# Two attention and GeGLU layers on one core: the second layer's first unit handled in two halves of its queries, other banks for dense products at the seam, new planner settings

## The chip, the core and the metric

The kernel runs on one core of a Trainium2 chip. Its engines each run their own instruction stream and meet through semaphores: TensorE (PE in the profile; its weight loads are shown as PEld) does the matrix products and writes PSUM, VectorE (DVE) and ScalarE (ACT) read PSUM, GpSimd (POOL) works on SBUF alone, and SyncE (SP) starts the DMAs. PSUM has eight banks of 512 fp32 columns. The metric is device time in microseconds of one launch; lower is better.

## What is computed

Two identical layers, each of attention with 32 heads of width 16 over 2048 tokens and a GeGLU feed-forward block. Everything is bf16 outside the accumulations.

```python
def _A_ref(x, wqkv, wo):          # H = 32, Dh = 16
    q, k, v = ...                 # x @ wqkv, split into heads
    scores = jnp.einsum("bhqd,bhkd->bhqk", q, k) * (Dh ** -0.5)
    p = _softmax(scores, axis=-1)
    o = jnp.einsum("bhqk,bhkd->bhqd", p, v)
    return o.transpose(0, 2, 1, 3).reshape(B, S, D) @ wo

def _B_ref(x, w_gate, w_up, w_down):
    return (_gelu(x @ w_gate) * (x @ w_up)) @ w_down

x = A_x                            # 1 x 2048 x 512; F = 1792
x = x + _A_ref(_layernorm(x), A_wqkv, A_wo)
x = x + _B_ref(_layernorm(x), B_w_gate, B_w_up, B_w_down)
x = x + _A_ref(_layernorm(x), A_wqkv, A_wo)
x = x + _B_ref(_layernorm(x), B_w_gate, B_w_up, B_w_down)
```

## The kernel before

**Units.** The queries of a layer are cut into blocks (four of 512 in the first layer; three of 512 and two of 256 in the second), the heads into eight groups of four. A block and a group make a unit. The four heads of a group lie in four row strips of 32 partitions, so a score product uses a quarter of PE's rows and two or four of them run side by side.

**Two passes.** A softmax subtracts the maximum of each row. The first pass finds it: `p1_emit` (L1636 matmul, L1651 DVE maximum) takes 128 queries, one key block of 512 and one head at a time, called a tile below; one maximum covers two tiles that lie in two neighbouring banks (128x1024) or a single one (128x512). A unit of 512 queries has 64 tiles, a layer 2048. When all tiles of a unit are done, `fin_step` reduces the four key blocks' maxima in six POOL steps (L1004 to L1009), DVE transposes the result (L1015), and `negmax` sends it by four small DMAs (L1031) into an extra row of QT, so that the second pass's scores come with the maximum subtracted. The second pass, `p2_tile` (L1518 matmul) and `p2_emit` (L1495 exponential on ACT, usually of two banks at once), makes the probabilities, and `pv_emit` (L1541) multiplies them with the values into bank 7; `nrm` divides by the sum. `QT`, `KT` and `KD` hold queries, keys and differences of two key blocks.

**Folds.** ACT can take a part of the first pass: `f_emit` (L1468 matmul with KD, L1475 ACT Relu) forms the positive part of a difference of two tiles, and DVE's L1646 adds it to the other tile while it takes the maximum, so that one 128x512 instruction serves two tiles.

**Dense products.** Projections, the output product and the feed-forward block are matmuls over all 128 rows (L759), made in runs of PIECE or GP matmuls between score matmuls. Each takes a free bank from `misc_banks` and is evicted by DVE or ACT; `pick` chooses (L774, L776). PE also issues filler matmuls on zeros (L1669) where it would stand idle.

**Banks.** The first pass owns banks 0 to 3, the second 4 to 6, the accumulator 7. While a dense product is open or could start, `p1_plan` is asked for its single form, in which the first pass uses the pair 0 and 1 and the single bank 2, and `misc_banks` hands out bank 3; where the second pass has nothing to do, 4 to 6 as well.

**The order** is worked out on the host: a planner (the loop at the end of `_build`) walks through time by estimates of each instruction's duration and emits the next instruction of every engine. Its choices are ruled by 19 settings (look-ahead, lag between the passes, size of runs, which engine evicts, and so on), which it takes from a row of PLAN; a new row is read after each 16 pairs of tiles (STRETCH).

**The seam between the layers.** The second layer's keys need the first layer's last feed-forward block. Therefore the first six units of the second layer (n_pre = 6) run over the first three key blocks of each group before any of them sees the fourth; `p1_turn` puts the rest in order of units as soon as the last key block of the first group is there. The first pass may be at most six units ahead of the second (n_ahead = 6), and the second pass can start only when the first unit is finished:

```python
if not p1_left[u]:                              # p1_emit
    fin_wait.append({"u": u, "stage": 0})
...
if u >= NU or u not in qp2_rec or gel["on"] is not None:   # p2_group
    return None
...
if pl is not None and (opened or fresh or wide) and not (gel["on"] is not None and (run or not fresh)):
    pl = p1_plan(now, True)
```

Here `can_p2` is false while the second pass has no unit to work on and `can_p1` true while the first pass has one; `gel["on"]` is set while the last block's gate products run with the Gelu on ACT; `pos["p1"]` counts pairs of tiles.

Of the kernel before, what the change touches and what calls it, by code (L numbers as in the profile page):

```python
# [11 lines left out]
AP = bass.AP  # L12
# [298 lines left out]
def _build(nc, x_in, wqkv, wo, wg, wu, wd, out, layer_blocks=((512, 512, 512, 512), (512, 512, 512, 256, 256)),  # L311
# [10 lines left out]
    NTT = S // 128  # L322
    NKB = S // 512
# [4 lines left out]
    with es:  # L328
# [138 lines left out]
        held = set()  # L467
# [1431 lines left out]
```

## Time and profile before

| | us |
|---|---|
| median of 3 runs | 2490.07 |
| lowest to highest | 2490.03 to 2490.46 |
| the profiled execution | 2490.04 |
| its span, first to last instruction | 2488.2 |

A profile's page gives one execution: the busy time of each engine and its share of the span, the span in 40 slices with the busy share of each in tenths, and the costliest groups of instructions. A group's row has the line, the engine, the operation, what it writes and reads with its shapes, the count, the busy time and the mean duration of one, and then the idle time just before it with what ended that. Rows of the timeline start with the start time and the duration of one or several merged instructions, of which the first one's shape is shown; a bracket holds the idle time before them and its releaser. Rows of busy time by stage hold the stretch, its length, and for each engine the busy time and the count. Some matmul records can be missing.

### The profile page before, as it was taken

How to read it: one execution, taken by the hardware profiler on the slowest of the kernel's cores; microseconds unless marked ns; L12 is line 12 of the kernel's file. 1: busy time of each engine (PE TensorE's matmuls, PEld its weight loads, DVE VectorE, ACT ScalarE, POOL GpSimd, SP SyncE). 2: the span in 40 equal slices, each digit the busy share in tenths (PEclk: the TensorE clock that was granted, in tenths of full speed). 3: DMA queues.
4: the chain of work that ended last, by engine and by line, in shares of the span. 5: the costliest groups of instructions: out<-in, count | busy, mean ns of one | idle time of the engine just before them, and what ended most of it. 6: DMA issues, size and time to landing. Idle time of an engine off the chain costs nothing.

```text
span 2488.2 us, 68820 instructions
## 1 busy us (share of the span) xinstructions
PE 2383.5 (96%) x29466; PEld 1145.1 (46%) x29720; DVE 2413.9 (97%) x3200; ACT 2340.4 (94%) x3190; POOL 1307.0 (53%) x2156
## 2 busy tenths in 40 slices
PE   8999999999999999999999999999999999999999
PEld 3444444444444444444433555554444444554456
DVE  9999999999999999999999999999999999999994
ACT  7999999999999999999965999999999999999996
POOL 5121238856788356877242211278617882269462
DMA  3110000000000000000000000000000000000000
GB/s 96 46 57 6 6 2 8 2 4 4 4 4 2 3 5 4 4 10 2 17 7 12 5 4 4 4 5 1 2 13 6 2 3 12 4 3 4 9 5 11
DMA packets 27354, 25.11 MB, mean 10 GB/s; under 512 B 9512, under 2 KB 26024, under 8 KB 27048
## 3 DMA queue, kind: packets, MB, share of 16 engines
q1 hardware_dynamic: 27048, 20.69, 2.9%
q8 instruction: 233, 3.82, 0.6%
q14 instruction: 73, 0.60, 0.1%
HBM read 9.70 MB, written 2.10 MB: 5 GB/s over the span
## 4 chain that ended last, share of the span: by engine, by line
DVE 41%; PE 36%; ACT 21%; issue 1%; POOL 0%; POOLq 0%; ACTq 0%; DVEq 0%
DVE PM L1651 39%; ACT SCR L1495 20%; PE PS L1636 12%; PE PS L759 9%; PE PS L1541 8%; PE PS L1518 3%; PE PS L1669 3%; DVE SCR L1646 1%; ACT SCR L1135 0%; ACT SCR L1475 0%; PE PS L881 0%; DVE HT L583 0%; PE PS L1468 0%; ACT AO L1209 0%; DVE AO L1229 0%
## 5 line engine op out<-in xcount | busy, mean ns | idle before, releaser
L1651 DVE TENSOR_REDUCE PM<-PS 128x2 f32<-128x1024 f32 (+1 forms) x2596 | 2234.8, 924 | 30.5 <-PE PS L1636 9.1
L1495 ACT ACTIVATE SCR<-PS 128x1024 bf16<-128x1024 f32 (+1 forms) x2484 | 2028.6, 910 | 69.0 <-PE PS L1518 47.3
L1636 PE MATMUL PS<-KT,QT 32*128 32x512 bf16 x3936 | 1047.0, 385 | 56.5 <-DVE PM L1651 33.4
L1518 PE MATMUL PS<-QT,KT 32*128 32x512 bf16 (+2 forms) x4736 | 945.7, 354 | 6.3 <-ACT SCR L1495 5.1
L1541 PE MATMUL PS<-VP,SCR 128*128 128x51 bf16 (+1 forms) x16384 | 811.3, 187 | 11.3 <-ACT SCR L1495 6.2
L1541 PEld LDWEIGHTS PS<-VP,SCR 128*128 128x128 bf16 x16384 | 573.5, 96 | 497.7 <-issue 421.7
L1636 PEld LDWEIGHTS PS<-KT,QT 32*128 32x128 bf16 x3936 | 249.7, 91 | 531.2 <-DVE PM L1651 328.8
L1669 PE MATMUL PS<-WV,ZER 128*128 128x240 bf16 x1948 | 365.7, 266 | 4.3 <-ACT SCR L1495 3.4
L1059 POOL TENSOR_TENSOR RL<-ACCS,CM 128x16 f32<-128x16 f32 (+2 forms) x66 | 179.4, 2718 | 339.9 <-ACT ACCS L1053 339.5
L1518 PEld LDWEIGHTS PS<-QT,KT 32*128 32x128 bf16 x4736 | 239.2, 91 | 65.9 <-ACT SCR L1495 41.2
L1004 POOL TENSOR_TENSOR PM<-PM 128x32 f32<-128x32 f32 (+2 forms) x74 | 18.0, 243 | 325.9 <-DVE PM L1651 320.6
L1669 PEld LDWEIGHTS PS<-WV,ZER 128*128 128x128 bf16 x1948 | 147.8, 96 | 61.7 <-issue 47.8
L1211 POOL TENSOR_TENSOR HT<-HT,AO 128x512 bf16<-128x512 bf16 x98 | 113.6, 1161 | 103.3 <-ACT AO L1209 102.6
L1248 POOL TENSOR_TENSOR KD<-KT 128x512 bf16<-128x512 bf16 x74 | 85.3, 1153 | 94.1 <-PE PS L1468 54.1
L759 PE MATMUL PS<-XNT,WU 128*128 128x512 bf16 (+2 forms) x499 | 124.4, 333 | 4.2 <-issue 2.9
L759 PE MATMUL PS<-XNT,WG 128*128 128x512 bf16 (+2 forms) x500 | 121.1, 333 | 5.1 <-issue 3.5
L759 PE MATMUL PS<-WD,HT 128*128 128x512 bf16 x384 | 121.2, 381 | 3.3 <-issue 1.4
L1139 POOL TENSOR_TENSOR HT<-HT,SCR 128x512 bf16<-128x512 bf16 (+1 forms) x98 | 106.2, 1083 | 4.7
L1133 POOL TENSOR_TENSOR SCR<-SCR,HT 128x512 bf16<-128x512 bf16 (+1 forms) x98 | 106.0, 1083 | 1.7
L1129 POOL TENSOR_TENSOR SCR<-HT 128x512 bf16<-128x512 bf16 (+1 forms) x98 | 95.8, 978 | 18.2 <-ACT HT L776 12.9
L1646 DVE CUSTOM_DVE_ANT_0 SCR<-PS,SCR 128x512 bf16<-128x512 f32 x160 | 102.7, 686 | 2.8 <-PE PS L1636 1.0
L1475 ACT ACTIVATE SCR<-PS 128x1024 bf16<-128x1024 f32 (+1 forms) x81 | 84.4, 1043 | 19.8 <-PE PS L1468 18.3
(128 smaller groups left out, 1509.1 us busy)
## 6 DMA issues: line engine op xcount, KB each, us to landing
KT<-SG SPq DMA_DIRECT2D x64, 64.0 KB
QT<-SG SPq DMA_DIRECT2D x56, 64.0 KB
QT<-MT SPq DMA_DIRECT2D x224, 1.0 KB
out_dram<-AO SPq DMA_DIRECT2D x16, 128.0 KB, 1.7
WG<-in_B_w_gate_dram SPq DMA_DIRECT2D x4, 448.0 KB, 3.8
WU<-in_B_w_up_dram SPq DMA_DIRECT2D x4, 448.0 KB, 4.8
WD<-in_B_w_down_dram SPq DMA_DIRECT2D x4, 384.0 KB, 4.5
HT<-in_A_x_dram SPq DMA_DIRECT2D x2, 512.0 KB, 8.9
```

Source lines behind the costliest of these rows:

```text
L759: ins = e.matmul(out_ap, lhsT=l, rhs=r_, start=(i == 0), stop=(i == n - 1))
L1059: emit("pool", lambda e: e.tensor_tensor(RL[:, s, 0:4 * nq], lsum, CM1[:, 0:4 * nq], op=ALU.pow), r=[("ACCS", s), ("CM1",)], w=[("RL", s)] ...
L1133: emit("pool", lambda e: e.tensor_tensor(u, u, ht, op=ALU.mult), r=[ku, kh], w=[ku], dur=0.18 + n / 520.0)
L1139: emit("pool", lambda e: e.tensor_tensor(ht, ht, u, op=ALU.mult), r=[ku, kh], w=[kh], dur=0.18 + n / 520.0)
L1211: emit("pool", lambda e, ft=ft, o=o: e.tensor_tensor(HV[:, ft, :], HV[:, ft, :], AO[:, o, 0:n], op=ALU.mult), r=[("AO", o)] + ht_keys(ft, ...
L1495: emit("act", lambda e: e.activation(dst, src, ACTF.Exp, scale=DH ** -0.5), r=[BK[bk + i] for i in range(cnt)], w=[("PT", i) for i in slot ...
L1518: ins = e.matmul(bank(bk)[:, i * n:(i + 1) * n], lhsT=KT[32 * j:32 * j + 32, g, kt * 128:(kt + 1) * 128], rhs=QT[32 * j:32 * j + 32, s, 0: ...
L1541: ins = e.matmul(acc, lhsT=PT[:, slot, i * n + qt * 128:i * n + (qt + 1) * 128], rhs=AP(VP, (kt * H + 4 * g + j) * 17, [[NTT * H * 17, 128 ...
L1636: ins = e.matmul(bank(b), lhsT=QT[32 * j:32 * j + 32, s, qt * 128:(qt + 1) * 128], rhs=KT[32 * j:32 * j + 32, g, kb * 512:(kb + 1) * 512], ...
L1646: emit("dve", lambda e, i=i, b=b, sl=sl: e.tensor_tensor_reduce(PT[:, sl, :], bank(b), PT[:, sl, :], 1.0, -3.0e38, ALU.add, ALU.max, po[:, ...
L1651: emit("dve", lambda e: e.tensor_reduce(po, PS[:, bs[0]:bs[0] + cnt, :], axis=AX.X, op=ALU.max), r=bks, w=[("PM", sm) + h[1:] for h in hs] ...
L1669: return e.matmul(PS[:, b, NACC:512], lhsT=ZER[:, :], rhs=WV[:, 0, 0:512 - NACC], start=(b != 7), stop=(b != 7), skip_group_check=True)
```

## The change

Three things are changed.

1. `qh` gives the number of parts in which a unit is finished: two (QH1) for the first unit of the second layer, one for all others. Tiles are counted per part, `fin_step` and `negmax` work on a part's queries, each part has its own key in the dependence tracking, and the second pass goes through that unit's first 256 queries and then through the others.
2. Past the 64th pair of tiles, while the second pass has nothing to work on, the first pass has, and no Gelu stretch is on, dense products take banks 4 to 6 only, and the first pass keeps its two pairs of banks.
3. 116 of PLAN's 128 rows are new; rows 2, 3, 6 to 11 and 13 to 16 stay.

```diff
 PLAN = [
-    (0.1, 0.0, 0.65, 0.42, 0.3, -0.1, 1, 1, 62, 84, 8, 80, 0.1, 2.0, 0, 2, 2, 2, 7),
-    (0.0, 0.0, 0.65, 0.42, 0.3, 0.05, 1, 1, 62, 160, 8, 80, 0.1, 2.0, 0, 2, 3, 2, 7),
+    (0.1, 0.0, 0.65, 0.42, 0.3, -0.1, 1, 1, 62, 6, 8, 80, 0.3, 2.0, 0, 2, 2, 2, 7),
+    (0.4, 0.05, 0.45, 0.22, 0.0, 0.0, 2, 2, 110, 36, 8, 80, 0.3, 4.0, 0, -6, 1, 4, 6),
...
@@ misc_banks
             if gel["on"] is not None and can_p1[0]:
                 bs = [5, 6] if GF else [4, 5, 6]
+            elif not can_p2[0] and can_p1[0] and pos["p1"] > 64:
+                bs = [4, 5, 6]
             elif not can_p2[0]:
                 bs += ([3] if bmode[0] else []) + [4, 5, 6]
@@ _build
+        qh = {u: 1 for u in range(NU)}
+        for la in range(1, NL):
+            qh[min(u for u in range(NU) if units[u][0] == la)] = QH1
+        qh_left = {(u, h): 16 * units[u][3] // 128 // qh[u] for u in range(NU) for h in range(qh[u])}
+        qh_done = {u: 0 for u in range(NU)}
+
+        def qkey(u, qt):
+            h = qt * qh[u] // (units[u][3] // 128)
+            return ("QT", u % n_qt, h) if h else ("QT", u % n_qt)
+
+        def p2_key(u):
+            return qkey(u, p2["h"] * (units[u][3] // 128) // qh[u])
+
+        def qh_count(u, qt):
+            h = qt * qh[u] // (units[u][3] // 128)
+            qh_left[u, h] -= 1
+            if not qh_left[u, h]:
+                fin_wait.append({"u": u, "stage": 0, "h": h})
@@ fin_step
-            nq = n // 128
-            pm = PM[:, s1, 0:nq * 4 * NKB].rearrange("p (a k) -> p a k", a=nq)
-            keys = [("PM", s1, qt, kb, j) for qt in range(nq) for kb in range(NKB) for j in range(4)]
+            nq = units[u][3] // 128 // qh[u]
+            q0 = f["h"] * nq
+            pm = PM[:, s1, q0 * 4 * NKB:(q0 + nq) * 4 * NKB].rearrange("p (a k) -> p a k", a=nq)
+            keys = [("PM", s1, qt, kb, j) for qt in range(q0, q0 + nq) for kb in range(NKB) for j in range(4)]
@@ negmax
-                        AP(QT, n_qt * 512 + sl * 512 + pg * 32, [[32 * n_qt * 512, 4], [128, nq], [1, 32]]),
+                        AP(QT, n_qt * 512 + sl * 512 + h * nq * 128 + pg * 32, [[32 * n_qt * 512, 4], [128, nq], [1, 32]]),
-            qp2_rec.add(u)
+            qh_done[u] += 1
+            if qh_done[u] == qh[u]:
+                qp2_rec.add(u)
@@ p2_group
-            if u >= NU or u not in qp2_rec or gel["on"] is not None:
+            if u >= NU or qh_done[u] <= p2["h"] or gel["on"] is not None:
                 return None
@@ p2_tile
-                                   rhs=QT[32 * j:32 * j + 32, s, 0:n], start=True, stop=True, tile_position=(32 * j, 0))
+                                   rhs=QT[32 * j:32 * j + 32, s, c0:c0 + n], start=True, stop=True, tile_position=(32 * j, 0))
@@ p1_emit
-            if not p1_left[u]:
-                fin_wait.append({"u": u, "stage": 0})
+            for h in hs:
+                qh_count(u, h[1])
@@ the planner's loop
-                if pl is not None and (opened or fresh or wide) and not (gel["on"] is not None and (run or not fresh)):
+                if pl is not None and (opened or fresh or wide) and not (gel["on"] is not None and (run or not fresh)) \
+                        and not (not can_p2[0] and gel["on"] is None and pos["p1"] > 64 and 3 not in held):
                     pl = p1_plan(now, True)
```

More of the change, by code (lines that the diff above doesn't have):

```diff
@@ L973, in qproj @@
                 sl = (u + i) % n_qt
-                keys = [("QT", sl)]
+                keys = [("QT", sl)] + [("QT", sl, h) for h in range(1, max(qh.values()))]
                 yield ("sp", [("SG", s)], keys)
@@ L1016, in fin_step, with negmax @@
                  r=[("MSEL", u % 2)], w=[("MT", u % 2)], dur=0.13)
-            fin_rec.add(u)
-            add(negmax(u), -1e6 + u)
+            if f["h"] == qh[u] - 1:
+                fin_rec.add(u)
+            add(negmax(u, f["h"]), -1e6 + u)
             f["stage"] = 9
             return True
-        def negmax(u):
+        def negmax(u, h):
             s1 = u % n_ahead
             sl = u % n_qt
-            nq = units[u][3] // 128
-            yield ("sp", [("MT", u % 2)], [("QT", sl)])
+            nq = units[u][3] // 128 // qh[u]
+            key = qkey(u, h * nq)
+            yield ("sp", [("MT", u % 2)], [key])
             def fn(e):
@@ L1366, in p2_group @@
             u = p2["u"]
-            if u >= NU or u not in qp2_rec or gel["on"] is not None:
+            if u >= NU or qh_done[u] <= p2["h"] or gel["on"] is not None:
                 return None
             if p2["todo"] is None:
-                p2["todo"] = [list(range(NTT * units[u][3] // 512)) for j in range(4)]
+                p2["todo"] = [list(range(NTT * units[u][3] // 512 // qh[u])) for j in range(4)]
             return u
@@ L1394, in p2_only @@
                 return []
-            tq = max(est([("QT", p2["u"] % n_qt)]), now)
+            tq = max(est([p2_key(p2["u"])]), now)
             left = p2_left()
@@ L1443, in f_opts @@
                     return []
-                tq = max(est([("QT", h[0] % n_qt), ("KD", h[0] % NKD)]), est(w=[("PT", so)]), now)
+                tq = max(est([qkey(h[0], h[1]), ("KD", h[0] % NKD)]), est(w=[("PT", so)]), now)
                 bs = (4,) if gel["on"] is not None else (6, 5) if wide else (6,)
@@ L1449, in f_opts @@
                 return []
-            tq = max(est([("QT", h[0] % n_qt), ("KD", h[0] % NKD)]), est(w=[("PT", sp), ("PT", sp + 1)]), now)
+            tq = max(est([qkey(h[0], h[1]), ("KD", h[0] % NKD)]), est(w=[("PT", sp), ("PT", sp + 1)]), now)
             return sorted((max(tq, est(w=[BK[b], BK[b + 1]])), b, 2, True) for b in ((3, 5) if wide else (4, 5))
@@ L1472, in f_emit @@
             bks = [BK[bk + d] for d in range(cnt)]
-            emit_pe(fn, 1, 512, r=[("QT", s), ("KD", sd)], w=bks, rows=[j + d for d in range(cnt)])
+            emit_pe(fn, 1, 512, r=[qkey(u, qt), ("KD", sd)], w=bks, rows=[j + d for d in range(cnt)])
             avoid.extend(j + d for d in range(cnt))
@@ L1498, in p2_emit @@
             if not p2_left():
-                p2_done.add(u)
-                p2["u"] += 1
+                p2["h"] += 1
                 p2["todo"] = None
+                if p2["h"] == qh[u]:
+                    p2_done.add(u)
+                    p2["u"] += 1
+                    p2["h"] = 0
         def p2_tile(u, avoid, bk, slot):
@@ L1508, in p2_tile @@
             kg = p2["todo"][j].pop(0)
+            c0 = p2["h"] * n // qh[u]
+            n //= qh[u]
             m = 512 // n
@@ L1518, in fn @@
                     ins = e.matmul(bank(bk)[:, i * n:(i + 1) * n], lhsT=KT[32 * j:32 * j + 32, g, kt * 128:(kt + 1) * 128],
[L1519 removed]
+                                   rhs=QT[32 * j:32 * j + 32, s, c0:c0 + n], start=True, stop=True, tile_position=(32 * j, 0))
                 return ins
[L1522 to L1523 removed]
+            emit_pe(fn, m, n, r=[p2_key(u)] + [("KT", g, kt // 4) for kt in kts], w=[BK[bk]], rows=[j])
+            return u, slot, j, kts, p2["h"]
         def pv_emit():
[L1526 removed]
+            u, slot, j, kts, h = pvq.pop(0)
             la, bi, t0, n, g = units[u]
+            nh = n // qh[u]
+            q0 = h * nh // 128
             first = u in pv_first
@@ L1535, in fn @@
                 for i, kt in enumerate(kts):
-                    for qt in range(nq):
+                    for qt in range(q0, q0 + nh // 128):
                         a = (qt * 4 + j) * 17
@@ L1540, in fn @@
                         acc = AP(PS, 7 * 512 + a, [[8 * 512, 128], [na - a, nb], [1, 17]])
-                        ins = e.matmul(acc, lhsT=PT[:, slot, i * n + qt * 128:i * n + (qt + 1) * 128],
+                        ins = e.matmul(acc, lhsT=PT[:, slot, i * nh + (qt - q0) * 128:i * nh + (qt - q0 + 1) * 128],
                                        rhs=AP(VP, (kt * H + 4 * g + j) * 17, [[NTT * H * 17, 128], [0, nb], [1, 17]]),
@@ L1639, in fn @@
                 return ins
-            emit_pe(fn, 1, 512, r=[("QT", s)] + kks, w=bks, rows=[h[3] for h in hs])
+            emit_pe(fn, 1, 512, r=[qkey(u, qt)] + kks, w=bks, rows=[h[3] for h in hs])
             po = AP(PM, sm * 16 * NKB + (qt * NKB + kb) * 4 + j0, [[n_ahead * 16 * NKB, 128], [1, cnt]])
```

15 lines of the change are left out of this document (6 added, 9 removed), and 226 rows, old and new, of the table PLAN.

## The prediction

> **What bounds the kernel now.** I read the page's head first, then busy time by stage, then the timeline of each engine at the seam between the layers.
>
> ```profile
> span 2488.2 us, 68820 instructions
> ...
> PE 2383.5 (96%) x29466; PEld 1145.1 (46%) x29720; DVE 2413.9 (97%) x3200; ACT 2340.4 (94%) x3190; POOL 1307.0 (53%) x2156
> ...
> ACT  7999999999999999999965999999999999999996
> ```
> ```profile
> 62.20:1240.00 1177.80, 1126.86 (x14053) 535.47 (x14173) 1168.50 (x1465) 1146.78 (x1560) 656.67 (x1094) 1.00 0.04 10
> ...
> 1368.00:1680.00 312.00, 305.56 (x4293) 159.66 (x4303) 305.43 (x396) 311.45 (x347) 102.56 (x191) 1.00 0.02 4
> 1680.00:2426.00 746.00, 714.64 (x9189) 344.12 (x9287) 735.22 (x933) 714.73 (x1031) 450.13 (x677) 1.00 0.02 5
> 2426.00:2488.20 62.20, 57.57 (x903) 39.77 (x907) 26.52 (x70) 43.56 (x82) 16.01 (x34) 1.00 0.03 11
> ```
>
> After the span the columns are PE, PEld, DVE, ACT, POOL. DVE (maxima of the first pass) and ACT (exponentials) share the bound. DVE is idle 9.3 us in the first long stage, 6.6 in the second, 10.8 in the third: 26.7 us over 2236. ACT is idle 31.0, 0.6 and 31.3 there. The large hole is the 6 and 5 in the ACT row: the seam. From 1368 to 1680 ACT is full and DVE has air; from 1680 on it is the other way round. So time won at the seam on ACT alone is worth its full size until 1680, and afterwards only as far as work can be moved from DVE to ACT.
>
> The profiled run took 2490.04 us, 1.84 over its span; the median of the three runs is 2490.07. The sum below starts from 2490.04.
>
> **The halves.** ACT's way out of the seam, then DVE, POOL, SP and PE on the same stretch:
>
> ```profile
> 1347.85 0.60 ACT L776 ACTIVATE VP<-PS 128x512 bf16<-128x512 f32 x1 [1.55 <-PE PS L759]
> 1348.47 1.28 ACT L1495 ACT_TABLE_LOAD   x1
> 1356.74 2.11 ACT L1495 ACTIVATE SCR<-PS 128x1024 bf16<-128x1024 f32 x2 [6.99 <-PE PS L1518]
> ```
> ```profile
> 1339.60 11.80 DVE L1651 TENSOR_REDUCE PM<-PS 128x2 f32<-128x1024 f32 x14 [1.79 <-PE PS L1636]
> 1351.32 0.20 DVE L1015 STREAM_TRANSPOSE MT<-MSEL 128x32 bf16<-128x32 bf16 x1
> ```
> ```profile
> 1349.22 0.25 POOL L1004 TENSOR_TENSOR PM<-PM 128x32 f32<-128x32 f32 x1 [15.78 <-DVE PM L1651]
> ...
> 1350.92 0.23 POOL L1009 TENSOR_TENSOR MSEL<-PM 128x16 bf16<-128x16 f32 x1
> 1358.58 0.25 POOL L1004 TENSOR_TENSOR PM<-PM 128x32 f32<-128x32 f32 x1 [7.43 <-DVE PM L1651]
> ```
> ```profile
> 1336.88 4.95 SPq L938 DMA_DIRECT2D KT<-SG  x8
> 1351.55 10.51 SPq L1031 DMA_DIRECT2D QT<-MT  x6
> ```
> ```profile
> 1356.27 0.39 PE L1518 MATMUL PS<-QT,KT 32*128 32x512 bf16 x2
> ```
>
> The last key block lands (SP), DVE takes unit 0's 16 tiles of 512 keys that lack it from 1339.60 until POOL starts at 1349.22, so 9.6 us or 0.60 a tile. POOL's six steps last to 1351.15, DVE transposes, SP issues four small DMAs at 1351.55, and the first score matmul of the second pass runs at 1356.27, 4.7 us after. With halves, eight tiles suffice: the chain starts 4.8 us earlier and the first exponential comes at 1356.74 − 4.8 = 1351.9. ACT's table load, done at 1349.75, and its last VP eviction, done at 1348.45, are still ahead of that, so neither is the next thing late. POOL's six steps on half the width I take at the same 1.9 us.
>
> What is added: a second set of six POOL steps (1.9 us; POOL stood idle 7.43 us there), one more transpose (0.20 us of DVE), four more DMAs. The SP queue is empty between the key transfers, over at 1341.83, and 1351.55. The second half is ready when the whole unit is now, 1356.7. By the exponential row (2.11 us for two) the first half's 16 exponentials take some 16 us from 1351.9, to 1368, so ACT does not run dry between the halves. One new wait: both halves share one MT buffer, so the second transpose waits until the first half's DMAs have read it. These start at 1346.7 and are through by 1351.4; the second transpose is due at 1351.3. DVE then stands 0.1 us, at worst about 1; queued behind it are maxima of unit 1, and until 1680 ACT does not wait for those. I charge 0.3 us with the transpose, inside the rounding.
>
> The exponentials of that unit now take 256 queries a matmul, so 128 score matmuls and weight loads instead of 64. The last units already have that shape, and PE has filler work (L1669) after the seam:
>
> ```profile
> 2331.64 0.12 PEld L1518 LDWEIGHTS PS<-QT,KT 32*128 32x128 bf16 x4
> ...
> 2331.64 0.39 PE L1518 MATMUL PS<-QT,KT 32*128 32x256 bf16 x4
> ```
> ```profile
> L1669 PE MATMUL PS<-WV,ZER 128*128 128x240 bf16 x380 | 73.1, 264 | 0.0
> ```
>
> Four of 256 take 0.39 us, as two of 512 do: no charge. If the cover were gone, 64 more loads at about 0.09 us would be 5.8 us of PE. [...]
>
> How much of 4.8 us reaches the end? Nothing, if DVE, whose work the halves don't shorten, sets it; all of it, if ACT does. In between, work moves: an eviction costs ACT 0.60 and DVE 0.68.
>
> ```profile
> L774 DVE CAST HT<-PS 128x512 bf16<-128x512 f32 x12 | 8.2, 682 | 0.3 <-PE PS L759 0.3
> ```
>
> If ACT takes w from DVE, ACT ends 4.8 − w earlier and DVE 1.13 w: equal at w = 2.25, which gives **2.5 us**. Bounds 0 and 4.8.
>
> **The banks.** At the seam the first pass now keeps banks 0 to 3, two pairs; dense products get 4 to 6. Before, an open dense product made it alternate pair and single.
>
> ```profile
> 1261.00:1279.00 18.00, 17.84 (x86) 5.54 (x85) 16.89 (x22) 9.37 (x16) 0.00 (x0) 1.00 0.00 1
> 1279.00:1302.50 23.50, 23.18 (x110) 6.08 (x111) 22.19 (x47) 17.45 (x25) 15.67 (x23) 1.00 0.00 1
> 1302.50:1326.00 23.50, 23.14 (x117) 7.67 (x120) 21.28 (x49) 12.74 (x16) 10.42 (x23) 1.00 0.03 7
> 1326.00:1339.50 13.50, 13.45 (x71) 4.68 (x69) 11.55 (x27) 7.79 (x14) 6.26 (x12) 1.00 0.05 13
> ```
> ```profile
> L1651 DVE TENSOR_REDUCE PM<-PS 128x2 f32<-128x1024 f32 x23 | 27.9, 1222 | 2.4 <-PE PS L1636 1.9
> ...
> L1475 ACT ACTIVATE SCR<-PS 128x1024 bf16<-128x1024 f32 x20 | 20.4, 1022 | 11.4 <-PE PS L1468 10.4 <-DVE PM L1646 0.5 <-PE PS L1636 0.4
> ...
> L1651 DVE TENSOR_REDUCE PM<-PS 128x1 f32<-128x512 f32 x23 | 15.6, 683 | 0.8 <-PE PS L1636 0.5 <-PE PS L1468 0.2
> ```
> ```profile
> 1341.53 0.38 PE L1636 MATMUL PS<-KT,QT 32*128 32x512 bf16 x1
> 1341.85 0.39 PE L759 MATMUL PS<-WV,XNT 128*128 128x512 bf16 x1
> 1342.17 0.39 PE L1636 MATMUL PS<-KT,QT 32*128 32x512 bf16 x2
> 1342.49 0.61 PE L759 MATMUL PS<-WV,XNT 128*128 128x512 bf16 x2
> ```
>
> From 1261 to 1339.5 PE is full, while DVE is idle 6.6 us and ACT far more: PE sets the pace. Between dense runs one score matmul costs PE 0.32 us from start to start, and a pair costs 0.32 as well. The 23 singles of this stretch, made into pairs, are 11.5 groups fewer: 11.5 × 0.32 = **3.7 us** of PE. Would DVE use it? Its maxima up to there:
>
> ```profile
> L1651 DVE TENSOR_REDUCE PM<-PS 128x2 f32<-128x1024 f32 x676 | 814.6, 1216 | 9.0 <-PE PS L1518 2.9 <-PE PS L1636 2.4
> L1651 DVE TENSOR_REDUCE PM<-PS 128x1 f32<-128x512 f32 x679 | 456.4, 680 | 3.7 <-PE PS L1636 1.0 <-PE PS L1518 0.2 <-PE PS L1468 0.2
> L1646 DVE CUSTOM_DVE_ANT_0 SCR<-PS,SCR 128x512 bf16<-128x512 f32 x152 | 97.5, 685 | 2.8 <-PE PS L1636 1.0 <-PE PS L1468 0.6 <-PE PS L1518 0.2
> ```
>
> 2 × 676 + 679 + 2 × 152 (a folded maximum serves two tiles) = 2335. The first layer has 2048, so 287 of the second are done, and the six early units have 6 × 48 = 288 tiles before the last key block. DVE ran out of tiles just as that block came; the 1.79 us before 1339.60 are that. So DVE and the dense chain end the seam together, and both gain only if the dense products come sooner, which freed PE time gives: 3.7 us, nearly all of it DVE idle time saved. Bounds: 6.6 us, all that DVE idles there; on the other side the loss of the third rival.
>
> **The settings.** No row prices them. They can fill DVE's 26.7 us of gaps and turn singles into pairs, or the reverse: by the maxima just shown a pair is 814.6 / 676 = 1.21 us busy and two singles are 2 × 456.4 / 679 = 1.34, so up to 0.13 us each. For sums of both signs I take 0; bounds below.
>
> Sum: 2490.04 − 2.5 − 3.7 = **2483.8 us**.
>
> **Rivals.**
> 1. *The lead is hidden.* DVE sets the end from 1680 on (735.22 of 746) and gets no tile sooner from the halves; of the banks only the 1.79 us wait goes. 2490.04 − 1.8 = 2488.2. For it: ACT already idles 31.3 us after 1680 unused. Against it: PE's full seam.
> 2. *The settings fill the middle.* Half of DVE's 26.7 us goes on top of the forecast: 2483.8 − 13.3 = 2470.5. For it: single maxima are more than half of all (679 of 1355 up to the seam). Against it: gaps of some 1.2% in three long stages are many small ones.
> 3. *Dense products and folds collide on banks 4 to 6, and the kernel is slower.* The 20 folds from 1261 to 1339.5 each hold two of the three banks for 0.39 + 1.02 us; a dense product holds one through its fill and an eviction of 0.60 us. Each collision that makes a dense product wait one eviction brings the last key block 0.60 us later. From eleven on both gains are gone; with all twenty it is 2483.8 + 12.0 = 2495.8. For it: one bank of four is taken. Against it: the up products run 14 times in the second of these windows, beside 11 folds:
>
> ```profile
> L1475 ACT ACTIVATE SCR<-PS 128x1024 bf16<-128x1024 f32 x11 | 11.2, 1022 | 2.7 <-PE PS L1468 2.2 <-DVE PM L1646 0.5
> ```
>
> A step of 23.5 / 14 = 1.68 us offers 5.0 bank-us; a dense product needs some 2.1 (two runs of two matmuls, 0.61 each, a score group of 0.32 between, the eviction) and the folds 2.2 (11 / 14 × 2 × 1.41): 86%, tight but enough.
> 4. *The settings lose.* About 108 pairs split into singles at 0.13 us each, 14 us: 2483.8 + 14 = 2497.8. For it: nothing in the trace holds the present mix in place. Against it: the same freedom can save as much.
>
> **How the numbers follow.** Forecast 0.32 (own range 2478 to 2487), first rival 0.20, second 0.22, third 0.14, fourth 0.12. A change under 0.2%, 5.0 us, cannot be told from none: the line is at 2485.1 and 2495.0. Faster: 0.27 of the forecast's 0.32, 0.03 of the first rival's, all of the second's 0.22: 0.52. Same: 0.05, 0.17, and 0.04 of the third and fourth together: 0.26. Slower: the other 0.22. The range runs from 2466, some 4 us beyond the second rival, to 2500, past the third and fourth; about 0.1 is left on each side.
>
> **What would show it.** Halves: POOL's six steps twice at half the width before the first exponential, which follows the landing of the last key block by 12.3 us in place of 17.1 (1339.60 to 1356.74). Banks: no singles among the maxima while dense products run at the seam, the last key block's maxima nearer to 1336 than 1339.6 if what lies before is unmoved, and DVE idle there under 3 us. Wrong: fewer than 15 folds in the stretch with ACT evictions waiting on PE (third rival); DVE's idle time after 1368 unchanged at 17 us and the end unmoved (first); or a difference that stands already before 1240, where only the settings act.

## The result, and the profile after

| | before | after |
|---|---|---|
| median of 11 runs on one chip, us | 2490.06 (2490.02 to 2490.76) | 2484.13 (2484.11 to 2484.18) |
| ratio to before, 95% interval | | 0.9976 [0.9968, 0.9984] |
| span of the profiled execution, us | 2488.2 | 2482.4 |

The page's head for the changed kernel: busy time, share of the span and instructions of each engine, and ACT's row of tenths in 40 slices.

```profile
span 2482.4 us, 69012 instructions
...
PE 2383.2 (96%) x29553; PEld 1146.8 (46%) x29802; DVE 2405.8 (97%) x3157; ACT 2344.6 (94%) x3210; POOL 1322.8 (53%) x2176
...
ACT  7999999999999999999976999999999999999997
```

Busy time by stage, in the same stages as before except the last, which ends with the span:

```profile
62.20:1240.00 1177.80, 1130.53 (x14059) 536.81 (x14175) 1166.02 (x1475) 1145.11 (x1549) 659.27 (x1097) 1.00 0.03 10
1240.00:1368.00 128.00, 123.69 (x821) 44.64 (x830) 121.89 (x216) 85.45 (x119) 50.92 (x105) 1.00 0.05 13
1368.00:1680.00 312.00, 304.09 (x4304) 158.46 (x4317) 302.39 (x386) 310.69 (x348) 107.13 (x195) 1.00 0.02 4
1680.00:2426.00 746.00, 717.44 (x9233) 347.28 (x9327) 732.03 (x902) 719.50 (x1057) 459.93 (x685) 1.00 0.02 5
2426.00:2482.40 56.40, 52.78 (x820) 36.50 (x822) 25.95 (x64) 38.38 (x75) 12.78 (x30) 1.00 0.03 11
```

By 1240 nothing is gained: the first layer's last exponential before the seam ends at 1230.2 before and at 1230.6 after. The hole of the seam in ACT's row is 7 and 6 in place of 6 and 5. After it DVE idles more than before, 9.6 and 14.0 us in the two long stages against 6.6 and 10.8. Yet the end is earlier.

The seam itself, in the timelines of ACT, DVE, POOL and SP (start, duration, instruction, count, idle time before it):

```profile
1344.00 0.60 ACT L797 ACTIVATE VP<-PS 128x512 bf16<-128x512 f32 x1 [0.69 <-PE PS L780]
1344.61 1.28 ACT L1520 ACT_TABLE_LOAD   x1
1349.75 1.94 ACT L1520 ACTIVATE SCR<-PS 128x1024 bf16<-128x1024 f32 x2 [3.86 <-PE PS L1548]
```
```profile
1337.86 6.88 DVE L1684 TENSOR_REDUCE PM<-PS 128x2 f32<-128x1024 f32 x6 [1.36 <-PE PS L1669]
1344.66 0.20 DVE L1036 STREAM_TRANSPOSE MT<-MSEL 128x32 bf16<-128x32 bf16 x1
...
1350.02 0.20 DVE L1036 STREAM_TRANSPOSE MT<-MSEL 128x32 bf16<-128x32 bf16 x1
```
```profile
1342.56 0.22 POOL L1025 TENSOR_TENSOR PM<-PM 128x16 f32<-128x16 f32 x1 [11.64 <-DVE PM L1684]
...
1344.14 0.20 POOL L1030 TENSOR_TENSOR MSEL<-PM 128x8 bf16<-128x8 f32 x1
1347.84 0.22 POOL L1025 TENSOR_TENSOR PM<-PM 128x16 f32<-128x16 f32 x1 [3.49 <-DVE PM L1684]
```
```profile
1344.89 7.57 SPq L1054 DMA_DIRECT2D QT<-MT  x8
```

POOL's steps run twice at half the width. The first starts 4.70 us after the last key block (1337.86 to 1342.56; before 9.62), and the first exponential comes 11.89 us after that block, before 17.14. So of the 6.99 us by which the exponentials resume sooner (1349.75 for 1356.74), 5.25 lie between the last key block and the first exponential, where the halves act, and 1.74 are an earlier key block. Of these 6.99 us, 5.80 are left at the end of the span.

The maxima from 1261 to the last key block, grouped by form (count, then busy time and mean ns, then idle time before), and all engines in four stages of that stretch, of which the sum is shown:

```profile
L1684 DVE TENSOR_REDUCE PM<-PS 128x2 f32<-128x1024 f32 x30 | 36.0, 1218 | 1.6 <-PE PS L1669 0.8
L1679 DVE CUSTOM_DVE_ANT_0 SCR<-PS,SCR 128x512 bf16<-128x512 f32 x42 | 26.5, 684 | 0.6 <-PE PS L1493 0.6
L1684 DVE TENSOR_REDUCE PM<-PS 128x1 f32<-128x512 f32 x11 | 7.4, 684 | 0.5 <-PE PS L1669 0.5
```
```profile
sum 76.00, PE 73.39 PEld 23.40 DVE 71.51 ACT 46.20 POOL 32.49; mean PE 18.35 PEld 5.85 DVE 17.88 ACT 11.55 POOL 8.12
```

Pairs went from 23 to 30 and singles from 23 to 11; the singles did not vanish, as the prediction had asked. PE, full before (77.6 of 78.5 us), now idles 2.6 of 76. DVE idles 4.5 us there, before 6.6; under 3 was asked.

### The profile page after: what moved, and what is told of

Read it like the earlier page. It is cut to its first block, busy times and chain, and to the rows that moved or that the text cites. A ratio compares the mean times of both kernels' runs of the same rounds, so it can differ in the third digit from the quotient of the medians.

```text
span 2482.4 us, 69012 instructions
## 1 busy us (share of the span) xinstructions
PE 2383.2 (96%) x29553; PEld 1146.8 (46%) x29802; DVE 2405.8 (97%) x3157; ACT 2344.6 (94%) x3210; POOL 1322.8 (53%) x2176
## 4 chain that ended last, share of the span: by engine, by line
DVE 40%; PE 36%; ACT 22%; issue 2%; POOL 0%; POOLq 0%; ACTq 0%; DVEq 0%
DVE PM L1684 38%; ACT SCR L1520 20%; PE PS L1669 12%; PE PS L780 9%; PE PS L1573 8%; PE PS L1548 4%; PE PS L1702 3%; DVE SCR L1679 1%; ACT SCR L1500 1%; ACT SCR L1160 0%; ACT AO L1234 0%; DVE HT L585 0%; PE PS L902 0%; PE PS L1493 0%; DVE AO L1254 0%
## 5 line engine op out<-in xcount | busy, mean ns | idle before, releaser
L1684 DVE TENSOR_REDUCE PM<-PS 128x1 f32<-128x512 f32 (+1 forms) x2585 | 2238.9, 929 | 38.6 <-PE PS L1548 16.2
L1520 ACT ACTIVATE SCR<-PS 128x1024 bf16<-128x1024 f32 (+1 forms) x2481 | 2026.1, 910 | 62.9 <-PE PS L1548 41.4
L1702 PE MATMUL PS<-WV,ZER 128*128 128x240 bf16 x1966 | 371.4, 265 | 3.6 <-issue 1.0
L1236 POOL TENSOR_TENSOR HT<-HT,AO 128x512 bf16<-128x512 bf16 (+1 forms) x109 | 121.3, 1115 | 86.1 <-ACT AO L1234 85.4
L1104 POOL TENSOR_TENSOR X<-X,AO 128x512 f32<-128x512 f32 x42 | 53.2, 1269 | 82.2 <-ACT AO L1102 81.8
```

The source lines that it names most:

```text
L1236: emit("pool", lambda e, ft=ft, o=o: e.tensor_tensor(HV[:, ft, :], HV[:, ft, :], AO[:, o, 0:n], op=ALU.mult), r=[("AO", o)] + ht_keys(ft, ...
L1520: emit("act", lambda e: e.activation(dst, src, ACTF.Exp, scale=DH ** -0.5), r=[BK[bk + i] for i in range(cnt)], w=[("PT", i) for i in slot ...
L1684: emit("dve", lambda e: e.tensor_reduce(po, PS[:, bs[0]:bs[0] + cnt, :], axis=AX.X, op=ALU.max), r=bks, w=[("PM", sm) + h[1:] for h in hs] ...
L1702: return e.matmul(PS[:, b, NACC:512], lhsT=ZER[:, :], rhs=WV[:, 0, 0:512 - NACC], start=(b != 7), stop=(b != 7), skip_group_check=True)
```

## Experiments

Three theories stood at first, and the expectations call them by these names. Seam theory: each edit has its own worth at the seam, and the rest of the kernel carries it to the end. Settings theory: the gain lies in the new rows. Scatter theory: any other order of work moves the end by several us either way. Every kernel's profile gives three numbers that part them: when DVE takes its first maximum over the last key block, when the second layer's first exponential starts, and how long it is from there to the end of the span.

| kernel | rows | last key block | first exponential | from it to the end | median, us |
|---|---|---|---|---|---|
| before | old | 1339.60 | 1356.74 | 1131.5 | 2490.06 |
| changed | new | 1337.86 | 1349.75 | 1132.7 | 2484.13 |
| halves alone | new | 1348.01 | 1360.19 | 1169.7 | 2531.64 |
| bank rule alone | new | 1338.64 | 1354.95 | 1171.3 | 2528.16 |
| neither | new | 1348.79 | 1365.31 | 1154.9 | 2520.06 |
| both edits | old | 1347.79 | 1359.21 | 1164.8 | 2525.36 |
| halves alone | old | 1339.76 | 1351.61 | 1142.8 | 2496.16 |
| bank rule alone | old | 1348.19 | 1364.77 | 1153.9 | 2519.11 |
| bank rule alone | refitted | 1337.85 | 1354.16 | 1147.0 | 2498.03 |
| halves alone | refitted | 1348.56 | 1360.66 | 1139.6 | 2501.54 |
| both edits, one number changed | new | 1338.45 | 1350.34 | 1142.3 | 2493.77 |

All but the median are of the profiled execution, which for the new settings alone is 2.1 us over its median and for the refitted bank rule 5.2.

**Without the halves.** The changed kernel with QH1 at 1.

```diff
-QH1=2):
+QH1=1):
```

> The changed kernel with its settings and its bank rule, but the first unit of the second layer finished as a whole (QH1=1). Seam theory: the gain is ACT's earlier return to exponentials (1349.75 against 1356.74 before), 1.7 us from an earlier last key block and 5.3 us from the halves, and ACT's lead reaches the end nearly in full. Then the first exponential comes some 5 us later than in the changed kernel, near 1355, and the time is 2484.1 + 5 = 2489. As the prediction had it (half of the lead lost to DVE): 2486.6. Settings theory (the gain lies in the new rows): 2484 to 2485. Scatter theory (any other order of the planner moves the end by several us either way): no relation between the first exponential and the end; anything from 2480 to 2500.

Measured: 2528.16 us, ratio to before 1.0154 [1.0137, 1.0171]. DVE's first maximum over the last key block and the first exponential:

```profile
1338.64 11.41 DVE L1684 TENSOR_REDUCE PM<-PS 128x2 f32<-128x1024 f32 x10 [1.36 <-PE PS L1669]
```
```profile
1354.95 1.94 ACT L1520 ACTIVATE SCR<-PS 128x1024 bf16<-128x1024 f32 x2 [6.99 <-PE PS L1548]
```

The first exponential is 5.20 us later, as seam theory had it, 0.78 of it with a later key block; the other 39 us of loss lie behind it, and no theory had those.

**Without the bank rule.** Both of its conditions are taken out of the changed kernel.

```diff
-            elif not can_p2[0] and can_p1[0] and pos["p1"] > 64:
-                bs = [4, 5, 6]
...
-                        and not (not can_p2[0] and gel["on"] is None and pos["p1"] > 64 and 3 not in held):
```

> The changed kernel with halves and new settings, dense products back on banks 2 or 3 too. Seam theory: the last key block's first maximum comes later than 1337.86, by the 1.7 us that it gained or by the predicted 3.7, and the end with it: 2485.8 to 2487.8; single maxima from 1261 to the last key block go from 11 back to some 23. Settings theory: 2484 to 2485. Scatter theory: anything.

Measured: 2531.64 us, ratio 1.0166 [1.0151, 1.0182]. DVE at the last key block:

```profile
1348.01 0.69 DVE L1682 TENSOR_REDUCE PM<-PS 128x1 f32<-128x512 f32 x1 [0.27 <-PE PS L1667]
```

The key block is 10.15 us later, where 1.7 to 3.7 were expected, and the first exponential 10.44; again most of the loss lies behind it.

**The new settings alone**, with neither edit: QH1 at 1 and the bank rule out.

```diff
-QH1=2):
+QH1=1):
...
-            elif not can_p2[0] and can_p1[0] and pos["p1"] > 64:
-                bs = [4, 5, 6]
...
```

> Only the new settings on the kernel before: no halves, no bank rule. Seam theory: all of the gain is gone, 2490 to 2491, first exponential at 1356 to 1358. Settings theory: 2484 to 2486. Scatter theory: anything, and likely slower than 2490, as the rows were not made for this order.

Measured: 2520.06 us, ratio 1.0117 [1.0102, 1.0132]. Among the new rows the two edits add up at the seam: 15.56 us for both, 5.12 for the halves (1365.31 to 1360.19) and 10.36 for the bank rule (1365.31 to 1354.95). They don't add up at the end: taking one edit out costs more than taking out both.

**Both edits with the old settings.** The changed kernel with PLAN of before.

```diff
 PLAN = [
-    (0.1, 0.0, 0.65, 0.42, 0.3, -0.1, 1, 1, 62, 6, 8, 80, 0.3, 2.0, 0, 2, 2, 2, 7),
+    (0.1, 0.0, 0.65, 0.42, 0.3, -0.1, 1, 1, 62, 84, 8, 80, 0.1, 2.0, 0, 2, 2, 2, 7),
...
```

> Halves and bank rule with the settings of before. Seam theory: the first exponential comes near 1350 and the end with it, 2484 to 2486. Settings theory: 2490. Scatter theory: the seam gains its 7 us, but the end does not follow; likely above 2490.

Measured: 2525.36 us, ratio 1.0148 [1.0131, 1.0165]. With rows that are not theirs the two edits make the kernel 35 us slower, and even the seam is 2.5 us later than before.

These four runs are 30 to 42 us slower than before. Seam and settings theory had nothing of the kind, and scatter theory, which spoke of several us, not the size. They led to a fourth reading, which the runs further down try: the settings are fitted to one exact order of work, so an edit is worth something only together with rows chosen for it. The table shows as much at the seam already. The last key block comes at 1338 to 1340 where the bank rule stands with rows made for it or neither is there, and at 1348 to 1349 wherever only one of the two is.

**ACT late, order kept.** 24 short instructions on ACT right before the second layer's first exponential; they are added when the order is already settled, so nothing else moves.

```diff
+            if u == 32 and not p2["h"] and p2_left() == 64 // qh[u]:
+                for _ in range(24):
+                    sch.op("act", lambda e: e.activation(SQ[:, 1, 0:1], CM05[:, 0:1], ACTF.Copy), r=[("CM05",)], w=[("SQ", 1, 0)])
```

> The changed kernel with its order of instructions, and 24 short activations (128x1 into a scratch word, each waiting for the one before, some 0.2 to 0.25 us, together about 5 us) put into ACT's stream ahead of the second layer's first exponential; the planner does not see them. If ACT sets the end from there on: the end comes later by nearly the whole delay, 2489. If the lead is shared half and half, as the prediction had it: 2486.6. If DVE sets the end: 2484 to 2485. Scatter theory in its strict form (any shift at the seam costs tens of us): 2510 and more; if only a changed order of instructions costs that, no more than the delay.

Measured: 2484.72 us, ratio 0.998 [0.9971, 0.999]. As a test it was too weak: most of the 5.59 us fell into ACT's 3.86 us of idle time, and the stream was back within 0.6 us at the third exponential (the last key block came 1.04 us later in this execution). By the medians the end is 0.6 us later, as much as the stream.

**DVE late, order kept.** The same place, 24 short instructions on DVE.

```diff
+                for _ in range(24):
+                    sch.op("dve", lambda e: e.tensor_scalar(SQ[:, 1, 1:2], CM05[:, 0:1], 1.0, None, op0=ALU.add), r=[("CM05",)], w=[("SQ", 1, 1)])
```

> The same with 24 short VectorE instructions in place of the activations, in DVE's stream at the same point of the plan, some 4 to 6 us, order otherwise that of the changed kernel. If ACT sets the end: under 1 us at the end, 2484 to 2485. Shared: 2486.6. If DVE sets the end from 1680 on: 2489.

Measured: 2493.05 us median, 2490.87 to 2500.53, ratio 1.0015 [1.0006, 1.0025]. PE's timeline (first row), DVE's (second), and busy time with the granted clock (the column 0.91, 0.50, 0.50, 0.99 behind POOL) in four stretches:

```profile
1356.18 0.58 PE L1672 MATMUL PS<-KT,QT 32*128 32x512 bf16 x1 [4.40 <-DVE PM L1687]
```
```profile
1366.89 0.20 DVE L1036 STREAM_TRANSPOSE MT<-MSEL 128x32 bf16<-128x32 bf16 x1
```
```profile
1353.00:1357.00 4.00, 0.81 (x3) 0.22 (x3) 3.58 (x14) 0.00 (x0) 0.00 (x0) 0.91 0.00 0
1357.00:1360.00 3.00, 3.00 (x30) 1.20 (x28) 2.37 (x3) 1.34 (x2) 0.00 (x0) 0.50 0.00 0
1360.00:1363.00 3.00, 3.00 (x38) 1.41 (x36) 1.92 (x3) 2.75 (x3) 0.00 (x0) 0.50 0.02 5
1363.00:1368.00 5.00, 5.00 (x88) 2.83 (x83) 4.72 (x8) 4.53 (x5) 1.49 (x6) 0.99 0.00 2
```

The 24 instructions hold DVE for 4.43 us, PE pauses 4.40 us for its banks, then runs at half the clock (0.50 from 1357 to 1363), and ACT starves behind PE: it waits 5.80 us for its third exponential. By its third transpose of the second layer DVE is 6.6 us late (1366.89 against 1359.84, with the last key block 0.42 us later), and the last exponential ends 6.7 us late by the same reckoning. Nothing of the delay is made up in the 1100 us that follow. The loss of 8.9 us by the medians is more than any theory had, DVE's included (2489).

**The halves alone, old settings.** The kernel before with the first part of the change only.

```diff
-LNPT1=8):
+LNPT1=8, QH1=2):
...
+            qh[min(u for u in range(NU) if units[u][0] == la)] = QH1
...
```

> Halves alone on the kernel before, with the settings of before. The first exponential comes some 5 us before 1356.7, at 1351 to 1352. Seam theory with a remainder as before (1131 us from there to the end): 2485. After the first four runs the remainder is expected 20 to 40 us longer, since the rows past the seam were not made for this order: 2505 to 2520.

Measured: 2496.16 us, ratio 1.0025 [1.0015, 1.0034]. The first exponential is 5.13 us earlier than before, and yet the kernel is 6 us slower; the time lies between the two that were expected. ACT's groups from 1525 to 1560 show where most of that went; first before, then this kernel:

```profile
L1495 ACT ACTIVATE SCR<-PS 128x1024 bf16<-128x1024 f32 x39 | 36.6, 1217 | 0.0
```
```profile
L1518 ACT ACTIVATE SCR<-PS 128x512 bf16<-128x512 f32 x34 | 19.5, 597 | 5.0 <-PE PS L1546 3.9
L1518 ACT ACTIVATE SCR<-PS 128x1024 bf16<-128x1024 f32 x12 | 11.5, 1217 | 0.0
```

In this stretch 34 exponentials cover a single bank. They take 3.6 us more than 17 pairs (19.5 against 17 × 36.6 / 39), and ACT waits 5.0 us for PE between them: 8.6 of the 11.3 us by which the remainder has grown. A likely reason is that the row of settings in force here was chosen for another state of the queues; no run changes that row alone.

**The bank rule alone, old settings.**

```diff
+            elif not can_p2[0] and can_p1[0] and pos["p1"] > 64:
+                bs = [4, 5, 6]
...
+                        and not (not can_p2[0] and gel["on"] is None and pos["p1"] > 64 and 3 not in held):
```

> The bank rule alone on the kernel before, with the settings of before. With both edits and these settings the first exponential came at 1359.2, so by addition this one gives 1364, later than before: the bank rule then costs some 8 us at the seam with these rows, where it won 10 us with the new ones (1365.3 to 1355.0). Remainder 20 to 40 us longer than before's 1131: 2515 to 2535. If the bank rule helps the seam whatever the rows, as the prediction took it: 1353.

Measured: 2519.11 us, ratio 1.0118 [1.0103, 1.0133]; the first exponential is 8.0 us later than before, both as expected by addition. DVE's timeline at the last key block:

```profile
1345.49 0.69 DVE L795 CAST SG<-PS 128x512 bf16<-128x512 f32 x1 [2.00 <-PE PS L780]
1348.19 10.27 DVE L1684 TENSOR_REDUCE PM<-PS 128x2 f32<-128x1024 f32 x9 [2.01 <-PE PS L1669]
```

The pairs are there (35 pairs and 22 singles from 1240 to 1338, before 27 and 29), but the last key block comes at 1348.19, 8.6 us late: a key projection is still being evicted at 1345.49. Pairs alone don't end the seam sooner; the dense chain must come in time too. With the new rows the same rule has its key block by 1338.64 or sooner.

**ACT later, order kept**, with 40 instructions, so that ACT is late by about what the halves are worth.

```diff
-                for _ in range(24):
+                for _ in range(40):
```

> The changed kernel in its own order of work, with 40 short ACT instructions in place of the 24 of the run with a late ACT, ahead of the second layer's first exponential. There 24 of them took 5.59 us, of which 3.86 us of idle time and the table load's place hid most: the first exponential came 1.6 us late against the changed kernel (1352.41 against 1349.75, the seam itself 1.05 us later in that execution), and from the third on the stream was only 0.6 us late. At 0.233 us each, 40 take 9.3 us, so here the first exponential comes some 5.3 us late, at about 1355, as without halves, and the stream 4.3 us late, with DVE's own work left alone. If in a fixed order every delay at the seam reaches the end one for one, on whichever engine it falls: 4.3 to 6 us over the changed kernel, 2488.4 to 2490.1 us. If DVE alone sets the end and only half of ACT's lead reaches it, as the prediction had it: 2.2 us, 2486.3 us. If ACT's lead is hidden: 2484.5 us. A fall of the granted clock while PE waits, as with the late DVE, would add 1 to 2 us to any of them.

Measured: 2493.10 us median, 2491.68 to 2500.42, ratio 1.0015 [1.0005, 1.0025]. ACT's first exponential, PE's longest pause, DVE just behind its second transpose, and the stages:

```profile
1356.10 2.85 ACT L1523 ACTIVATE SCR<-PS 128x1024 bf16<-128x1024 f32 x3
```
```profile
1357.18 0.61 PE L1551 MATMUL PS<-QT,KT 32*128 32x256 bf16 x4 [3.63 <-ACT SCR L1523]
```
```profile
1358.79 1.22 DVE L1687 TENSOR_REDUCE PM<-PS 128x2 f32<-128x1024 f32 x1 [4.51 <-PE PS L1672]
```
```profile
1353.00:1357.00 4.00, 0.55 (x3) 0.09 (x1) 1.27 (x3) 3.76 (x10) 0.00 (x0) 0.88 0.00 0
1357.00:1360.00 3.00, 2.82 (x30) 1.23 (x32) 1.22 (x1) 2.31 (x4) 0.00 (x0) 0.50 0.00 0
1360.00:1363.00 3.00, 3.00 (x37) 1.37 (x36) 1.92 (x3) 2.72 (x3) 0.00 (x0) 0.52 0.02 5
```

The first exponential is 5.4 us late (1356.10, with the last key block 0.98 us later). DVE, which was given nothing to do, stands 4.51 us for PE, and PE 3.63 us for ACT. It is the same picture as with the late DVE, the clock included, and the same 9 us at the end. This tells against "DVE sets the end and takes half": in a settled order the engines are one chain. In the profiled execution the last exponential ends 6.25 us late by the same reckoning, within the 4.3 to 6 us of the delay and the 1 to 2 allowed for the clock. That execution is the shortest of the ten; the median's 9.0 us go with a lower mean clock (0.997 for 0.998), in executions of which no trace was kept.

**The bank rule alone, refitted**, and **the halves alone, refitted**: as without the halves and without the bank rule, but with 68 and 65 of the later rows of PLAN chosen anew by the planner's own reckoning.

```diff
-QH1=2):
+QH1=1):
...
 PLAN = [
...
```

> The bank rule without the halves, as in the run without halves, but with the settings of the 68 stretches from the 60th on chosen anew for it: single values and rows were changed one after the other and kept where the planner's own reckoning of the end came out lower. Computation and seam edits are those of the run without halves (2528.16 us; first exponential 1354.95, and 1171 us from it to the end of the span, against 1132.65 in the changed kernel). If the settings are fitted to one order of work and the loss of that run was misfit: the stretch from the first exponential to the end falls to 1135 to 1150 us and the time to 2490 to 2506 us, still over the changed kernel by the 5 us of the halves and by what so short a fitting leaves. If the loss came from finishing the unit in one piece itself, beyond the 5 us at the seam, new rows change little: over 2518 us.

```diff
-            elif not can_p2[0] and can_p1[0] and pos["p1"] > 64:
-                bs = [4, 5, 6]
...
 PLAN = [
...
```

> The halves without the bank rule, as in the run without the bank rule (2531.64 us; first exponential 1360.19, 1169.7 us from it to the end), with the settings of 65 stretches from the 62nd on chosen anew in the same way. Fitted settings: 2490 to 2508 us, with the first exponential back at about 1350 to 1356 and 1135 to 1150 us after it; the seam's 10.4 us that the bank rule was worth among the unfitted rows then shrinks to a few us. If the bank rule were itself worth 10 us at the seam in any order: the first exponential stays at 1359 to 1361 and the time over 2510 us.

Measured: 2498.03 us, ratio 1.0043 [1.0026, 1.006], and 2501.54 us, ratio 1.0046 [1.0031, 1.0061]. Other numbers in the same code took back 30 us of each one's loss, all of it behind the first exponential, which stayed within 0.8 us of where it was. For the halves that is a miss: the seam did not come back to 1350 to 1356, so these rows did not mend what the bank rule's absence does there. The times lie where fitted settings were expected to bring them. Both are still over the kernel before, so they don't say what either edit is worth at its best. (The profiled execution of the refitted bank rule, 2503.18 us, lies 5 us over its median; its granted clock is 0.97 from 1450 to 1680.)

**One setting.** The changed kernel with the first value of row 78 altered, which is read only behind the seam.

```diff
-    (0.2, 0.15, 0.45, 0.62, 0.1, -0.05, 2, 1, 30, 92, 8, 60, 0.7, 1.0, 10, 6, 2, 1, 5),
+    (0.6, 0.15, 0.45, 0.62, 0.1, -0.05, 2, 1, 30, 92, 8, 60, 0.7, 1.0, 10, 6, 2, 1, 5),
```

> The changed kernel with both edits and one number of its 2432 settings changed: the first value of row 78 from 0.2 to 0.6, which is read some 80 us after the second layer's first exponential. The seam and everything before it stay as they are (first exponential 1349.75). If settings are fitted to one order and any departure scrambles what follows: 2490 to 2515 us, with the loss spread over the stretch behind that row. If rows are robust, so that the losses of the runs with one edit or with the other rows belong to the edits: 2483.5 to 2485 us.

Measured: 2493.77 us, ratio 1.0017 [1.0007, 1.0026], 9.6 us over the changed kernel. Busy time from 1680 to 1840, the changed kernel and then this one (DVE is the third time, ACT the fourth):

```profile
1680.00:1760.00 80.00, 77.07 (x883) 34.42 (x895) 78.44 (x99) 77.84 (x115) 73.76 (x84) 1.00 0.01 2
1760.00:1840.00 80.00, 76.35 (x958) 35.09 (x967) 79.86 (x97) 75.45 (x100) 21.07 (x25) 1.00 0.03 10
```
```profile
1680.00:1760.00 80.00, 79.27 (x838) 33.85 (x835) 76.80 (x97) 73.61 (x112) 73.07 (x84) 1.00 0.01 2
1760.00:1840.00 80.00, 78.84 (x922) 35.06 (x921) 75.78 (x90) 74.03 (x100) 24.53 (x31) 1.00 0.03 10
```

DVE and ACT are each 5.7 us less busy here, well behind the place where that row is read. No edit is responsible for a loss of this kind. It fits the fourth reading, in which a different order meets rows that were chosen for another state; which of the later rows does it was not tried.

## Why the prediction came out right, and where it did not

**The time** was right, 2483.8 for 2484.13, but that it is so close is luck: three terms were off and nearly cancelled. Booked by place, from the spans, the runs give 2488.2 − 5.25 (from the key block to the first exponential, where 2.5 was taken for the halves) − 1.74 (the key block, where 3.7 was taken for the banks) + 1.19 (a longer remainder, where 0 was taken for the settings) = 2482.4. Whether the 1.19 us are a cost of the settings or a part of the lead that did not arrive, no run tells.

**The halves at the seam**: the mechanism held, and the size, 4.8 us, lies inside what was measured. Counted from the last key block, so that an earlier or later one does not enter, the first exponential follows after 11.42 to 12.18 us in every kernel with halves and after 16.31 to 17.14 in every kernel without. Between kernels that differ in the halves alone they give 5.29 and 5.16 us with the old rows, 4.42 and 4.34 with the new. So some 0.8 of the 5.25 us belongs to the new order: the whole unit needs 16.31 us there too. POOL's narrower steps saved nothing, as the prediction took it: from its first step to the issue of the DMAs it is 2.33 us before and after. From that issue to the first exponential it is 4.86 us in place of 5.19. The second half's transpose starts while DVE still has maxima, at 1350.02, right behind them, so the wait on the shared MT buffer costs nothing. Score matmuls over 256 queries, charged at nothing, took 0.39 us for four at 1349.31, with their four weight loads covered (0.12 us from the same start), and brought no loss that the seam shows.

**The half that reaches the end** is the step that failed: "If ACT takes w from DVE, ACT ends 4.8 − w earlier and DVE 1.13 w: equal at w = 2.25". It takes the end for a balance of two busy times, and DVE for the engine that ends last because it is the fuller from 1680 on; so 2.5 of 4.8 us were to arrive. 5.80 of 6.99 did. The tail shows where DVE ends. The last maxima of before and of the changed kernel:

```profile
2433.18 2.41 DVE L1651 TENSOR_REDUCE PM<-PS 128x1 f32<-128x512 f32 x3
```
```profile
2435.35 1.82 DVE L1684 TENSOR_REDUCE PM<-PS 128x2 f32<-128x1024 f32 x2 [0.26 <-PE PS L1548]
```

Their last exponentials, with the table load for the Gelu behind them:

```profile
2459.14 5.83 ACT L1495 ACTIVATE SCR<-PS 128x1024 bf16<-128x1024 f32 x7 [0.23 <-PE PS L1518]
2464.99 1.28 ACT L1156 ACT_TABLE_LOAD   x1
```
```profile
2451.94 7.00 ACT L1520 ACTIVATE SCR<-PS 128x1024 bf16<-128x1024 f32 x9 [0.41 <-PE PS L1548]
2458.96 1.28 ACT L1181 ACT_TABLE_LOAD   x1
```

Before, exponentials go on for 29.4 us after DVE's last maximum (2435.6 to 2465.0); after, for 21.8 (2437.2 to 2459.0). DVE finishes 1.6 us later and the kernel 5.8 us earlier, so DVE's last maximum did not set the end. (Its maxima do pace the middle: of the chain that ended last they make 50% between 1680 and 2120 before, and 65% after.)

All engines from the first exponential to that table load, before and after:

```profile
1356.74:2464.99 1108.25, 1068.36 (x14243) 532.90 (x14357) 1067.95 (x1372) 1071.86 (x1438) 569.64 (x905) 1.00 0.02 5
```
```profile
1349.75:2458.96 1109.21, 1071.79 (x14349) 535.75 (x14462) 1067.77 (x1336) 1077.56 (x1465) 581.33 (x915) 1.00 0.02 5
```

Work did move from DVE to ACT, and far more than w = 2.25: 24 more evictions of dense products, 12 us, lie on ACT here. By the prediction's rule that would have made ACT end later. It ended 6.03 us earlier: 6.99 from the seam, less 5.70 of added busy time, plus 4.74 of idle time saved. DVE's busy time stayed the same, since it took more maxima for the evictions that it lost. So the sums of busy time did not set the end. The order-keeping runs add that in a fixed order a lateness at the seam, put on either engine, reaches the end as it stood at the third transpose, to within 0.3 us. What the lead alone would bring stays open, as the two changes behind the seam are nearly as large as it is and nearly cancel.

**The banks**: 3.7 us was predicted from 11.5 groups fewer in the stretch from 1261 on. Singles and pairs together went from 46 to 41, five fewer, which at 0.32 us is 1.6. Of the 1.74 us by which the key block came sooner, 0.69 stood already ahead of that stretch (the table load for the Gelu starts at 1260.34 in place of 1261.03), so 1.05 were gained in it. The price is not shown either: with the old rows the rule brings more pairs and a key block 8.6 us later, with the new rows its absence makes it 10.15 us later. The rule and the rows gain 1.74 us together; what the rule alone is worth stays open.

**The settings** were taken as 0. PLAN has 129 rows, of which 13 stay (counted from 0: 2, 3, 6 to 12 and 14 to 17). The reasoning, small gaps of both signs, missed what they are: not a tuning on top of the edits but a condition of them. With the old rows, or with new ones made for both edits, each edit alone is 6 to 42 us slower than before.

**The rivals.** The lead was not hidden. The middle was not filled: DVE idles 23.6 us there, before 17.4. The dense products did not collide with the folds: 20 folds on ACT from 1261 on as before, and an earlier key block. "The settings lose" was priced as 108 pairs of maxima split (by the prediction's rows at 0.14 us each, not 0.13); with the new rows pairs became more, 1201 for 1180 in the whole run. Splitting is what the old rows did to the halves alone, but of exponentials, in a lump of 34 singles in one place.

## What to carry to other kernels

The engine that is fullest in a long stage need not be the one that ends last; look for the last instruction of each, and at how long the other goes on alone. With an order fixed ahead, a delay at a point where every engine meets moved all that followed by its whole size (with the late DVE 6.6 us at the third transpose and 6.7 at the last exponential); that a gain does so by itself was not run. And where settings have been fitted to such an order, an edit's worth can't be read from a run that keeps the old settings: compare at the place of the edit, and fit anew before judging the end.

## What the runs showed of the hardware

A pause of PE that the mean clock of the execution hardly shows (0.998 in the runs with DVE late and with ACT later) cost more than its length. In these two PE paused for 4.40 and 3.63 us; the granted clock was 0.91 and 0.88 from 1353 to 1357, 0.50 to 0.52 from 1357 to 1363, and 0.99 and 1.00 from 1363 to 1368, while the changed kernel has 1.00 in each of these stretches. At the low clock the same score matmul took 0.58 to 0.61 us in place of 0.39. With the late DVE, 4.43 us of delay had become 6.6 us by the third transpose at 1366.89. Executions of that one kernel ranged from 2490.87 to 2500.53 us, while the changed kernel's lay within 0.07 us; the profiled one was among the shorter (span 2489.5, mean clock 0.998), and the longest had a span of 2498.8 at 0.992. Not all scatter is of this kind: the first run with a late ACT, in whose trace PE idles 1.4 us in all from 1330 to 1368, at a clock of 1.00, has one execution of 2490.20 us among nine of at most 2485.59, at a mean clock of 0.997.
